# Copying v on VectorE and GpSimd, and reordering the opening of a windowed-attention and gated-MLP kernel

## The chip, the cores and the metric

The kernel runs on one core of a Trainium2 chip. The metric is the device time of one execution in microseconds (us): the median of the timed runs. A core has five engines that work side by side, each through its own instructions in order: TensorE (PE in the profile; PEld are its weight loads), VectorE (DVE), ScalarE (ACT), GpSimd (POOL) and SyncE (SP), whose queue here only starts DMA transfers. PE reads SBUF and writes PSUM banks. GpSimd starts transfers too: all loads that convert f32 to bf16 stand in its instruction stream, between its arithmetic.

## The reference

Sliding-window causal attention (8 batches, 8 heads, 576 positions, 64 per head, window 64), whose output, as 4608 rows of 512, goes through a gated two-layer product:

```python
    scores = scale * np.matmul(q, k.transpose(0, 1, 3, 2))
    rel = pos[:, None] - pos[None, :]
    mask = (rel >= 0) & (rel < window)
    ...
    attn = np.exp(scores - max)
    attn = attn / (np.sum(attn, axis=-1, keepdims=True) + 1e-09)
    x = np.matmul(attn, v)            # heads side by side: 4608 x 512
    h = x @ w_in                      # 512 x 2048
    g = h * np.cos(h)
    return g @ w_out                  # 2048 x 512
```

## The kernel before, in words

**Tiles.** Attention works on units of 64 queries against 128 keys. A unit is (batch b, pair of heads p, block j of 64 positions, 0 to 8). The two heads of a pair lie in partitions 0 to 63 and 64 to 127. Up to four units form a group: groups 0 to 7 are batch 0's blocks 0 to 7 (two groups for each of four pairs, called p.g), group 8 is batch 0's block 8 of all pairs, groups 9 to 16 are batch 1's blocks 0 to 3 (odd numbers) and 4 to 6 (even), two for each pair; 17 and 18 are batch 1's blocks 7 and 8. The gated product works on row tiles of 512 rows; row tile 0 is batch 0's blocks 0 to 7, row tile 1 is group 8 with groups 9 to 16.

**Steps of a group.** Scores on PE (g_scores; L277 writes the mask for the first eight groups, L287 and L293 the products), maximum on VectorE (g_max, L303 and L307), exponentials with their row sums on ScalarE (g_exp, L318), reciprocal on VectorE (g_inv, L325), normalisation on GpSimd or VectorE (g_norm, L332, which writes w), then the transpose of w: by PE and a copy (L341, g_put) for the groups in `direct` (0 to 7, 8, 15, 16), by a DMA transpose that SP issues for the others (L344). `values` (L359) and `values_half` (L378) multiply with v, put_x copies the result to xT.

**v.** load_v (L183) puts 128 positions of v into every second slot of vtiles. A block whose 128 keys straddle two loads needs the odd slots, whose halves are copies from the neighbours. spread_v makes them: for each half of the partitions one strided copy, by an SP DMA (engine "s", L194) or by an engine's copy ("d" VectorE, "p" GpSimd, through `copy`, L132). For batch 0, zA copies slot 1, zB slots 3 and 5, zC slot 7 (each for one or both halves); for batch 1, step y does all at once, y.0 the lower half of the partitions (3 slots) and y.1 the upper (4 slots).

**Order.** Nothing is scheduled by the compiler: the order of the program text is the order on each engine. The string FIRST (L48) writes out the opening by hand, up to about 63 us, and the loop at L534 runs it. Step names: Lq, Lk, Lv, Lwi, Lwo are loads (batch or quarter of the weights, piece); tq, tk transpose batch 0's q and k of a pair on PE, pq, pk copy them out (last letter: the engine, a for ScalarE, d for VectorE, p for GpSimd); Tq, Tk, Pq, Pk the same for batch 1; ms clears a block tile on VectorE; s, m, e, i, n, w, c are the steps of group p.g; Gs, Gm, Ge, Gi, Gn, Gw/Gc, Gp those of a group by number; v and x are values and put_x for half of row tile 0 (x.1.0 is pairs 2 and 3 of the first half); h, S, g are the first product (L392), the sine (L398) and the gate (L404), 16 of each, five PSUM banks between them in turn (the last number of h is the bank); o and oc are quarters of the second product and its copy out (L411); V and X are values and put_x of row tile 1; tb and tb2 load ScalarE's sine and exp tables. Row tile 1 and all later ones run in the loop at L540, into which a planner (`at`, `pump`) mixes the attention of the batches to come. There the first product is L428, the sine L556, the gate L559 and the second product L570.

**Around the change.** GpSimd's stream in the opening is: loads of q and k, loads of v, three of w_in's four quarters (Lwi.0 to Lwi.2), seven normalisations, Lwi.3, the last normalisation n.3.1, then w_out, the rest of batch 1 and q, k of batch 2, mixed with the normalisations of groups 9 to 14 and 8. A load waits until the load eight places before it has landed. SP's stream is: two loads of q and k, the copies zB.0, zB.1, zC (L194), the transposes of w of groups 10 and 9, the copy y.0, the transposes of groups 12, 11, 14, 13, 17, 18, then transposes of batch 2's k (L247).

The steps that the prediction uses: h.0.4 is the first product's first step on the third quarter of w_in, h.0.6 the first on the fourth; V.2 is the values of pair 2 in row tile 1, which needs groups 13 and 14.

Of the kernel before, what the change touches and what calls it, by code (L numbers as in the profile page):

```python
# [10 lines left out]
def _safe_warn(msg, *a, **kw):  # L11
# [37 lines left out]
    "io ms.0.d Lq0.0 Lk0.0 ms.1.d mk cq.d ms.2.d mc ck.a tq.0 Lq0.1 pq.0.d Lk0.1 tk.0 pk.0.a s.0.0.0 "  # L49
    "Lq0.2 tq.1 tk.1 m.0.0 pq.1.a ms.3.d s.0.1.1 Lk0.2 tq.2 pk.1.d s.1.0.2 Lq0.3 Lk0.3 tk.2 s.1.1.3 "  # L50
    "e.0.0 tq.3 m.0.1 Lq1.0 Lk1.0 Lq1.1 pq.2.d pk.2.d Lk1.1 tk.3 m.1.0 s.2.0.4 Lv0.0 Lv0.1 Tq.0 Lv0.2 "
    "pk.3.d m.2.0 e.0.1 pq.3.a i.0.0 e.1.0 Tk.0 s.3.0.0 Tq.1 e.2.0 Lv0.3 Lwi.0 Pq.0.d i.1.0 Lwi.1 m.3.0 "
    "m.1.1 i.2.0 Pk.0.a e.3.0 Lwi.2 Tk.1 n.1.0.p s.2.1.1 Pq.1.d Gs.10.2 m.2.1 Gs.9.4 n.0.0.p Pk.1.a "
    "n.2.0.p i.3.0 e.1.1 w.0.0 zA.0.d w.1.0 c.0.0.d Gs.12.0 w.2.0 n.3.0.p i.0.1 c.1.0.d zA.1.d c.2.0.d "
    "e.2.1 zB.0.s zB.1.s n.0.1.p i.1.1 w.3.0 v.0.0 c.3.0.d x.0.0.a s.3.1.3 Gm.10 v.1.0 m.3.1 i.2.1 "
    "Gs.11.2 Gm.9 Gm.12 n.1.1.p x.1.0.a e.3.1 ms.4.d w.0.1 w.1.1 c.1.1.a i.3.1 h.0.0.1 h.0.1.4 tb "
    "n.2.1.p c.0.1.d Lwi.3 w.2.1 h.0.2.0 n.3.1.p v.0.1 S.0.0 Gm.11 w.3.1 S.0.1 h.0.3.3 Lwo.0 S.0.2 "
    "c.2.1.d c.3.1.d v.1.1 zC.s g.0.0 S.0.3 h.0.4.2 ms.5.d x.0.1.a x.1.1.d h.0.5.1 g.0.1 h.1.0.4 g.0.2 "
    "g.0.3 S.0.4 ms.6.d h.0.6.0 h.1.1.3 S.0.5 S.1.0 Lq1.2 S.0.6 g.0.4 S.1.1 g.1.0 h.1.2.2 Lk1.2 ms.7.d "
    "Lq1.3 h.0.7.4 g.0.5 h.1.3.1 Lv1.0 Lwo.1 g.1.1 S.1.2 h.1.4.3 g.0.6 Lk1.3 S.0.7 h.1.5.0 g.1.2 h.1.6.2 "  # L60
# [13 lines left out]
def kernel(  # L74
# [10 lines left out]
    B, H, S, D = q.shape  # L85
# [45 lines left out]
    def copy(engine, out, in_):  # L131
        {"a": nc.scalar.copy, "p": nc.gpsimd.tensor_copy}.get(engine, nc.vector.tensor_copy)(out, in_)  # L132
# [54 lines left out]
    def spread_v(b, half, engine="p", lo=0, hi=4):  # L187
        vt = vtiles[b % 2]
        hi = min(hi, 4 - (half == 0))
        d = slice(64 * half, 64 * half + 64)  # L190
        of = 2 * lo + 2 * (half == 0)
        to, of = vt[d, 2 * lo + 1:2 * hi:2], vt[d, of:of + 2 * (hi - lo) - 1:2]
        if engine == "s":
            nc.sync.dma_start(out=to, in_=of)  # L194
        else:
            copy(engine, to, of)
# [102 lines left out]
    def g_max(n):  # L299
        s_ps, units = st["s", n], groups[n]  # L300
        negm = att.tile([128, GF], F32, tag="negm", name="negm", bufs=8)
        if n < n_first:
            nc.vector.tensor_reduce(out=negm[:, 0:len(units)], in_=s_ps, op=ALU.max, axis=AX.X, negate=True)  # L303
        else:
            s = att.tile([128, GF, 128], F32, tag="s", name="s", bufs=4)
            for u, (b, p, j) in enumerate(units):
                nc.vector.tensor_tensor_reduce(out=s[:, u], in0=s_ps[:, u], in1=mask[:, 2 - j % 2 if j else 0],  # L307
                                               scale=-scale if b else -1.0, scalar=BIG, op0=ALU.add, op1=ALU.min,
                                               accum_out=negm[:, u:u + 1])
            st["s", n] = s  # L310
        st["m", n] = negm
# [152 lines left out]
    n = n_listed  # L464
# [45 lines left out]
    def spread_first(lo, hi):  # L510
        return lambda i, engine: spread_v(0, i, engine, lo, hi)
# [28 lines left out]
    for mt in range(1, n_mt):  # L540
# [5 lines left out]
        for ff in range(n_ff):  # L546
# [8 lines left out]
            e = ff % 2  # L555
# [54 lines left out]
```

## Time and profile before

| | us |
|---|---|
| median of 3 timed runs (lowest, highest) | 313.28 (312.45, 314.71) |
| the profiled execution | 313.61 |
| its span in the trace | 311.8 |
| PE busy | 296.8 (95%) |
| DVE busy | 230.6 (74%) |
| ACT busy | 236.1 (76%) |
| POOL busy | 191.7 (61%) |

The granted clock of TensorE is full throughout (1.00). In the first 60 us the DMA engines are busy in nearly every slice, and PE's busy share is below 10 in 10 only there: 5.25 of the first 10 us, 7.25 of the next, 9.62, 9.95, 9.54, then 8.24 from 50 to 60. How to read it: a line of the chain gives start, length, engine and line of what the end of the execution waited for at that time; a line of waits gives who waited for whom, the total, how often and the longest; a line of the timeline gives start, length, engine, line, operation and how many were merged. "SPq" rows are the times in which SP issued a transfer, not the transfer.

### The profile page before, as it was taken

The page shows a single profiled execution, that of the slowest core. Times are in us where ns is not written, and L with a number is a line of the kernel's source. Part 1 is how long each engine was busy: PE and PEld are TensorE (multiplying, and loading weights), DVE is VectorE, ACT ScalarE, POOL GpSimd, SP SyncE. Part 2 cuts the span into 40 slices and gives each one's busy share as a digit, 9 for nine tenths or more (in the row PEclk, how much of TensorE's full clock was granted, in tenths as well). Part 3 has the DMA queues.
Part 4 walks back from the last instruction along what each step waited for, and adds up shares of the span by engine and source line. Part 5 has one row for each costly group of instructions (what it writes and reads, how often), then busy time and mean ns, then how long its engine had stood idle before and what let it go on. Part 6 is the DMA issues. An engine that isn't in the chain of part 4 may idle for free.

```text
span 311.8 us, 7954 instructions
## 1 busy us (share of the span) xinstructions
PE 296.8 (95%) x2627; PEld 161.6 (52%) x2659; DVE 230.6 (74%) x877; ACT 236.1 (76%) x785; POOL 191.7 (61%) x227
## 2 busy tenths in 40 slices
PE   3789999799999999999999999999999999999996
PEld 3667844445555455445545545455545554454443
DVE  5898978489777976798579867987698758335801
ACT  5998799486997799769976997699869986116600
POOL 8988576993569678966997699769902850000000
PEclk9999999999999999999999999999999999999999
DMA  7999999999959996999999998999794333011011
GB/s 150 175 212 187 200 178 132 132 162 167 241 82 113 138 235 84 117 116 230 120 105 129 216 138 94 139 230 120 91 135 155 65 80 141 0 69 68 0 67 70
DMA packets 155162, 41.17 MB, mean 132 GB/s; under 512 B 143280, under 2 KB 150384, under 8 KB 155120
## 3 DMA queue, kind: packets, MB, share of 16 engines
q0 software_dynamic: 100192, 18.06, 80.8%
q1 hardware_dynamic: 54784, 22.40, 38.1%
q8 instruction: 21, 0.34, 0.5%
q14 instruction: 21, 0.17, 0.2%
q10 hardware_dynamic: 144, 0.20, 0.2%
HBM read 36.70 MB, written 9.44 MB: 148 GB/s over the span
## 4 chain that ended last, share of the span: by engine, by line
PE 83%; DMA 8%; ACT 3%; POOL 3%; DVE 1%; issue 1%; SPq 1%; POOLq 0%; DVEq 0%; ACTq 0%
PE h_ps L428 34%; PE out_ps L570 34%; DMA w_in<-in_moe_w_in_dram 4%; PE s_ps L287 4%; PE h_ps L392 3%; PE o_ps L359 3%; ACT e L318 2%; PE tq_ps L214 2%; DMA wT<-w 2%; DMA k<-in_k_dram 2%; POOL v L183 1%; PE out_ps L440 1%; PE out_ps L411 1%; DVE s L307 1%; SPq L344 1%
## 5 line engine op out<-in xcount | busy, mean ns | idle before, releaser
L570 PE MATMUL out_ps<-w_out,gT 128*128 128x512 bf16 x482 | 116.1, 379 | 0.8 <-issue 0.2
L428 PE MATMUL h_ps<-xT,w_in 128*128 128x512 bf16 x498 | 115.2, 379 | 1.0
L556 ACT ACTIVATE sin<-h_ps 128x512 f32<-128x512 f32 x128 | 74.0, 598 | 34.0 <-PE h_ps L428 30.8
L318 ACT ACTIVATE e<-s,negm 128x128 f32<-128x128 f32 x256 | 98.7, 388 | 0.7 <-DVE negm L307 0.6
L559 DVE TENSOR_TENSOR gT<-h_ps,sin 128x512 bf16<-128x512 f32 x128 | 81.6, 685 | 21.4 <-ACT sin L556 20.6
L332 POOL TENSOR_TENSOR w<-e,rden 128x512 bf16<-128x512 f32 (+1 forms) x75 | 71.2, 965 | 38.7 <-DVE rden L325 36.9
L428 PEld LDWEIGHTS <-w_in 128*128 128x128 bf16 x512 | 48.6, 98 | 53.9 <-issue 0.4
L570 PEld LDWEIGHTS <-gT 128*128 128x128 bf16 x496 | 45.9, 98 | 44.2
L307 DVE CUSTOM_DVE_ANT_0 s<-s_ps,mask 128x128 f32<-128x128 f32 x256 | 58.5, 286 | 1.2 <-PE s_ps L293 1.0
L318 ACT ACTIVATION_READ_ACCUMULATOR e<-s,negm 128x1 f32 x256 | 48.1, 188 | 0.0
L177 POOL DMA_DIRECT2D q<-in_q_dram x36 | 29.0, 805 | 11.1 <-DMA v<-in_v_dram 4.3
L183 POOL DMA_DIRECT2D v<-in_v_dram x40 | 34.1, 873 | 0.4 <-DMA q<-in_q_dram 0.3
L177 POOL DMA_DIRECT2D k<-in_k_dram x36 | 28.8, 802 | 6.9 <-DMA k<-in_k_dram 5.6
L325 DVE RECIPROCAL rden<-den 128x4 f32<-128x4 f32 (+1 forms) x79 | 13.7, 173 | 21.0 <-ACT e L318 17.2
L132 ACT COPY out_sb<-out_ps 128x512 f32<-128x512 f32 (+1 forms) x18 | 10.2, 565 | 24.5 <-PE out_ps L570 18.4
L287 PEld LDWEIGHTS <-qB 128*128 128x128 bf16 x216 | 17.1, 98 | 14.2
L132 DVE CAST xT<-o_ps 128x512 bf16<-128x512 f32 x24 | 15.6, 677 | 10.8 <-PE o_ps L359 10.8
L132 DVE COPY out_sb<-out_ps 128x512 f32<-128x512 f32 x18 | 12.4, 689 | 13.5 <-PE out_ps L570 12.4
L132 DVE COPY qB<-tq_ps 64x576 bf16<-64x576 bf16 x48 | 21.6, 450 | 0.3
L287 PE MATMUL s_ps<-kT,qB 128*128 128x128 bf16 x216 | 21.9, 219 | 0.0
L307 DVE DVE_READ_ACCUMULATOR2_ANT negm<- 128x1 f32 x256 | 21.3, 83 | 0.0
L132 POOL COPY v<-v 64x1536 bf16<-64x1536 bf16 (+1 forms) x10 | 16.8, 1676 | 0.3
(64 smaller groups left out, 253.2 us busy)
## 6 DMA issues: line engine op xcount, KB each, us to landing
out_dram<-out_sb SPq DMA_DIRECT2D x16, 512.0 KB, 7.8
v<-in_v_dram POOLq DMA_DIRECT2D x32, 128.0 KB, 6.1
q<-in_q_dram POOLq DMA_DIRECT2D x36, 96.0 KB, 8.9
k<-in_k_dram POOLq DMA_DIRECT2D x36, 96.0 KB, 9.0
w_in<-in_moe_w_in_dram POOLq DMA_DIRECT2D x4, 512.0 KB, 9.2
w_out<-in_moe_w_out_dram POOLq DMA_DIRECT2D x4, 512.0 KB, 11.3
wT<-w SPq DMA_TRANSPOSE x68, 4.1
q<-in_q_dram POOLq DMA_DIRECT2D x7, 144.0 KB, 6.2
```

The lines of the kernel that those rows point to most:

```text
L132: {"a": nc.scalar.copy, "p": nc.gpsimd.tensor_copy}.get(engine, nc.vector.tensor_copy)(out, in_)
L177: nc.gpsimd.dma_start(out=st[name, b][:, c].rearrange("p (h d) -> p h d", h=H), in_=src.rearrange("h p d -> p h d"))
L183: nc.gpsimd.dma_start(out=vt.rearrange("p (h d) -> p h d", h=H), in_=v[b, :, c * 128:c * 128 + n, :].rearrange("h p d -> p h d"))
L287: nc.tensor.matmul(out=s_ps[:, u].rearrange("p (a t) -> p a t", a=2), lhsT=qblocks[(b % 2) * PAIRS + p][:, j].rearrange("d h t -> d (h t)" ...
L307: nc.vector.tensor_tensor_reduce(out=s[:, u], in0=s_ps[:, u], in1=mask[:, 2 - j % 2 if j else 0], scale=-scale if b else -1.0, scalar=BIG, ...
L318: nc.scalar.activation(e[:, u], s[:, u], AF.Exp, bias=negm[:, u:u + 1], scale=1.0 if n < n_first else -1.0, accum_out=den[:, u:u + 1])
L325: nc.vector.reciprocal(out=rden[:, 0:len(groups[n])], in_=den[:, 0:len(groups[n])])
L332: (nc.gpsimd if engine == "p" else nc.vector).tensor_tensor(out=w[:, 0:u], in0=e[:, 0:u], op=ALU.mult, in1=rden[:, 0:u].unsqueeze(2).to_br ...
L428: nc.tensor.matmul(out=st["h", ff], lhsT=w_in_sb[:, ks, ff * 128:ff * 128 + 128], rhs=st["xT", mt][:, ks], start=start, stop=stop)
L556: nc.scalar.activation(sin, h_ps, AF.Sin, bias=math.pi / 2.0)
L559: nc.vector.tensor_tensor(out=gt[:, e], in0=h_ps, in1=sin, op=ALU.mult)
L570: nc.tensor.matmul(out=o_ps[e], lhsT=gT[ff // 2][:, ff % 2, ms * 128:ms * 128 + 128], rhs=w_out_sb[:, ff], start=ff == 0, stop=ff == n_ff - 1)
```

## The change

The v copies that SP issued as DMA in the opening become copies on engines: zB.0, zB.1 and zC on VectorE (they stand elsewhere in the string, zB one behind the other's work), y.0 on GpSimd in two pieces, yA (two slots) and yB (one slot), with a normalisation between them. The scores and exponentials of the fourth pair's first group (s.3.0, m.3.0, e.3.0) come before batch 1's first k transposes (Tk.0) and copy; that copy, Pk.0, moves from ScalarE to VectorE. Normalisation n.0.0 stands before Lwi.1; n.1.0, n.2.0 and n.3.0 before Lwi.2. v.0.0 stands before w.3.0, and clearing ms.4 later, among the gates. The instructions after the opening are the same in the same order.

```diff
@@ -49,24 +49,24 @@
     "io ms.0.d Lq0.0 Lk0.0 ms.1.d mk cq.d ms.2.d mc ck.a tq.0 Lq0.1 pq.0.d Lk0.1 tk.0 pk.0.a s.0.0.0 "
     "Lq0.2 tq.1 tk.1 m.0.0 pq.1.a ms.3.d s.0.1.1 Lk0.2 tq.2 pk.1.d s.1.0.2 Lq0.3 Lk0.3 tk.2 s.1.1.3 "
     "e.0.0 tq.3 m.0.1 Lq1.0 Lk1.0 Lq1.1 pq.2.d pk.2.d Lk1.1 tk.3 m.1.0 s.2.0.4 Lv0.0 Lv0.1 Tq.0 Lv0.2 "
-    "pk.3.d m.2.0 e.0.1 pq.3.a i.0.0 e.1.0 Tk.0 s.3.0.0 Tq.1 e.2.0 Lv0.3 Lwi.0 Pq.0.d i.1.0 Lwi.1 m.3.0 "
-    "m.1.1 i.2.0 Pk.0.a e.3.0 Lwi.2 Tk.1 n.1.0.p s.2.1.1 Pq.1.d Gs.10.2 m.2.1 Gs.9.4 n.0.0.p Pk.1.a "
-    "n.2.0.p i.3.0 e.1.1 w.0.0 zA.0.d w.1.0 c.0.0.d Gs.12.0 w.2.0 n.3.0.p i.0.1 c.1.0.d zA.1.d c.2.0.d "
-    "e.2.1 zB.0.s zB.1.s n.0.1.p i.1.1 w.3.0 v.0.0 c.3.0.d x.0.0.a s.3.1.3 Gm.10 v.1.0 m.3.1 i.2.1 "
-    "Gs.11.2 Gm.9 Gm.12 n.1.1.p x.1.0.a e.3.1 ms.4.d w.0.1 w.1.1 c.1.1.a i.3.1 h.0.0.1 h.0.1.4 tb "
-    "n.2.1.p c.0.1.d Lwi.3 w.2.1 h.0.2.0 n.3.1.p v.0.1 S.0.0 Gm.11 w.3.1 S.0.1 h.0.3.3 Lwo.0 S.0.2 "
-    "c.2.1.d c.3.1.d v.1.1 zC.s g.0.0 S.0.3 h.0.4.2 ms.5.d x.0.1.a x.1.1.d h.0.5.1 g.0.1 h.1.0.4 g.0.2 "
-    "g.0.3 S.0.4 ms.6.d h.0.6.0 h.1.1.3 S.0.5 S.1.0 Lq1.2 S.0.6 g.0.4 S.1.1 g.1.0 h.1.2.2 Lk1.2 ms.7.d "
-    "Lq1.3 h.0.7.4 g.0.5 h.1.3.1 Lv1.0 Lwo.1 g.1.1 S.1.2 h.1.4.3 g.0.6 Lk1.3 S.0.7 h.1.5.0 g.1.2 h.1.6.2 "
-    "Lwo.2 g.0.7 S.1.3 S.1.4 S.1.5 Lwo.3 h.1.7.4 Lv1.1 S.1.6 g.1.3 g.1.4 S.1.7 g.1.5 Lv1.2 g.1.6 tb2 "
-    "Tk.2 Lv1.3 Pk.2.d Ge.10 Tq.2 Pq.2.d Tq.3 Ge.9 Ge.12 o.0.0.1 Pq.3.d Tk.3 o.1.0 Pk.3.d Lv0.4 Lq2.0 "
-    "Ge.11 Gs.14.3 Gi.10 Gm.14 g.1.7 Lq2.1 Gs.13.0 Lq2.2 o.0.1.2 Gi.9 o.2.0 Ge.14 Gn.10.p Gm.13 Gc.10 "
-    "Gi.12 Gs.8.3 o.1.1 Gs.16.4 Gm.8 o.3.0 Ge.13 o.2.1 Gs.15.0 Gi.11 oc.0.d Gn.9.p o.3.1 Gn.12.p o.0.2.3 "
-    "Gi.14 Gm.15 Gs.17.1 oc.1.d Gc.9 y.0.s Gn.11.p Gi.13 Gm.16 o.1.2 Ge.8 Ge.16 Ge.15 y.1.d Gn.14.p Gi.8 "
-    "Gc.12 Gm.17 o.0.3.0 Gi.16 Gn.13.p Gc.11 Gn.8.p Lq2.3 Lq2.4 Lq2.5 o.2.2 Gn.16.d Gw.8 Gc.14 Gc.13 "
-    "Lk2.0 Gp.8.d o.3.2 Gi.15 Gw.16 Lk2.1 Ge.17 Lk2.2 o.1.3 Gn.15.d V.0 Gp.16.d oc.2.a Gw.15 Gi.17 Lk2.3 "
-    "o.2.3 V.1 Gp.15.d X.0.a Gn.17.d X.1.d V.2 V.3 X.2.a X.3.d Gc.17 o.3.3 oc.3.a Gs.18.4 Gm.18 Ge.18 "
-    "Lk2.4 Gi.18 Gn.18.d Gc.18 Lk2.5 Lv1.4 "
+    "pk.3.d m.2.0 e.0.1 pq.3.a i.0.0 e.1.0 s.3.0.0 Tk.0 Tq.1 e.2.0 Lv0.3 Lwi.0 m.3.0 Pq.0.d i.1.0 "
+    "n.0.0.p Lwi.1 m.1.1 i.2.0 e.3.0 Pk.0.d Tk.1 n.1.0.p s.2.1.1 Pq.1.d Gs.10.2 m.2.1 Gs.9.4 Pk.1.a "
+    "n.2.0.p i.3.0 e.1.1 w.0.0 zA.0.d w.1.0 c.0.0.d Gs.12.0 w.2.0 n.3.0.p Lwi.2 i.0.1 c.1.0.d zA.1.d "
+    "c.2.0.d e.2.1 n.0.1.p i.1.1 v.0.0 w.3.0 c.3.0.d x.0.0.a s.3.1.3 Gm.10 v.1.0 m.3.1 zB.0.d i.2.1 "
+    "Gs.11.2 Gm.9 Gm.12 n.1.1.p x.1.0.a e.3.1 w.0.1 w.1.1 c.1.1.a i.3.1 h.0.0.1 h.0.1.4 tb n.2.1.p "
+    "c.0.1.d zB.1.d Lwi.3 w.2.1 h.0.2.0 n.3.1.p v.0.1 S.0.0 Gm.11 w.3.1 S.0.1 h.0.3.3 Lwo.0 S.0.2 "
+    "c.2.1.d c.3.1.d v.1.1 g.0.0 S.0.3 h.0.4.2 ms.5.d x.0.1.a x.1.1.d h.0.5.1 g.0.1 h.1.0.4 g.0.2 g.0.3 "
+    "ms.4.d S.0.4 ms.6.d h.0.6.0 h.1.1.3 S.0.5 S.1.0 Lq1.2 S.0.6 g.0.4 S.1.1 g.1.0 zC.d h.1.2.2 Lk1.2 "
+    "ms.7.d Lq1.3 h.0.7.4 g.0.5 h.1.3.1 Lv1.0 Lwo.1 g.1.1 S.1.2 h.1.4.3 g.0.6 Lk1.3 S.0.7 h.1.5.0 g.1.2 "
+    "h.1.6.2 Lwo.2 g.0.7 S.1.3 S.1.4 S.1.5 Lwo.3 h.1.7.4 Lv1.1 S.1.6 g.1.3 g.1.4 S.1.7 g.1.5 Lv1.2 g.1.6 "
+    "tb2 Tk.2 Lv1.3 Pk.2.d Ge.10 Tq.2 Pq.2.d Tq.3 Ge.9 Ge.12 o.0.0.1 Pq.3.d Tk.3 o.1.0 Pk.3.d Lv0.4 "
+    "Lq2.0 Ge.11 Gs.14.3 Gi.10 Gm.14 g.1.7 Lq2.1 Gs.13.0 Lq2.2 o.0.1.2 Gi.9 o.2.0 Ge.14 Gn.10.p Gm.13 "
+    "Gc.10 Gi.12 Gs.8.3 o.1.1 Gs.16.4 Gm.8 o.3.0 Ge.13 o.2.1 Gs.15.0 Gi.11 oc.0.d Gn.9.p o.3.1 Gn.12.p "
+    "o.0.2.3 Gi.14 Gm.15 Gs.17.1 oc.1.d Gc.9 Gn.11.p Gi.13 Gm.16 o.1.2 Ge.8 Ge.16 Ge.15 y.1.d Gn.14.p "
+    "yA.p Gi.8 Gc.12 Gm.17 o.0.3.0 Gi.16 Gn.13.p yB.p Gc.11 Gn.8.p Lq2.3 Lq2.4 Lq2.5 o.2.2 Gn.16.d Gw.8 "
+    "Gc.14 Gc.13 Lk2.0 Gp.8.d o.3.2 Gi.15 Gw.16 Lk2.1 Ge.17 Lk2.2 o.1.3 Gn.15.d V.0 Gp.16.d oc.2.a Gw.15 "
+    "Gi.17 Lk2.3 o.2.3 V.1 Gp.15.d X.0.a Gn.17.d X.1.d V.2 V.3 X.2.a X.3.d Gc.17 o.3.3 oc.3.a Gs.18.4 "
+    "Gm.18 Ge.18 Lk2.4 Gi.18 Gn.18.d Gc.18 Lk2.5 Lv1.4 "
 )
 
 
@@ -522,6 +522,7 @@
              "pq": lambda p, engine: put_q(0, p, engine), "pk": lambda p, engine: put_k(0, p, engine),
              "Pq": lambda p, engine: put_q(1, p, engine), "Pk": lambda p, engine: put_k(1, p, engine),
              "zA": spread_first(0, 1), "zB": spread_first(1, 3), "zC": lambda engine: spread_v(0, 1, engine, 3, 4),
+             "yA": lambda engine: spread_v(1, 0, engine, 0, 2), "yB": lambda engine: spread_v(1, 0, engine, 2, 3),
              "y": lambda half_, engine: spread_v(1, half_, engine),
              "s": lambda p, g, which: g_scores(2 * p + g, which), "m": lambda p, g: g_max(2 * p + g),
              "e": lambda p, g: g_exp(2 * p + g), "i": lambda p, g: g_inv(2 * p + g),
```

## The prediction

> **What bounds the kernel now.** I read the page's shares first, then the chain of waits in order of time, then the waits of PE by stretch, then the timeline of the queue that the chain passes through. All times below are microseconds from the span's start in the one profiled execution (313.61 us, span 311.8; the median of the timed runs, 313.28, lies 0.33 below it).
>
> The page's chain gives 83% to PE and 8% to DMA; the last two lines are PE's waits from 64 us on and its DMA and POOL waits before 65:
>
> ```profile
> PE 83%; DMA 8%; ACT 3%; POOL 3%; DVE 1%; issue 1%; SPq 1%; POOLq 0%; DVEq 0%; ACTq 0%
> ...
> PE out_ps L570 <- issue: 0.2, 1, 0.2
> ...
> PE o_ps L359 <- DMA wT<-w: 1.5, 1, 1.5
> PE out_ps L411 <- DMA w_out<-in_moe_w_out_dram: 0.3, 1, 0.3
> PE h_ps L392 <- DMA w_in<-in_moe_w_in_dram: 0.2, 1, 0.2
> ```
>
> After 64 us PE waits 0.2 us in all, so nothing there can be gained; what the change moves lies before it, and a shift of the point where the second row tile's loop begins (59.9) passes whole to the end. The chain up to there, in order of time (start, length, what):
>
> ```profile
> 13.48 13.31 DMA w_in<-in_moe_w_in_dram
> 26.84 10.65 PE h_ps L392 x96
> ...
> 49.20 1.05 POOL w L332
> 50.25 0.59 SPq L344
> 50.93 1.21 SPq L344
> 52.22 5.68 DMA wT<-w
> 57.95 0.66 PE o_ps L359 x30
> ```
>
> The reader sees two places where PE is released from outside: 26.84, the third part of w_in (waited for 0.2 us), and 57.95, the transposed weights of group 13 (1.5 us). The second is a queue: the normalised tile was done at 50.25, its transpose was issued only at 52.22, because the transposes of groups 12, 11, 14 and 13 go out one behind another at about 1.3 us each from 48.30. Why they begin so late stands in SP's timeline and SP's waits:
>
> ```profile
> 43.78 2.58 SPq L344 DMA_TRANSPOSE wT<-w  x2
> 47.60 0.60 SPq L194 DMA_DIRECT2D v<-v  x1
> 48.30 15.94 SPq L344 DMA_TRANSPOSE wT<-w  x6
> ...
> SPq L194 <- DMA v<-in_v_dram: 16.8, 2, 15.7
> ```
>
> Step y.0.s (batch 1's v, moved by DMA) stands on SP between the second and third transpose and waits for loads of v that land at 47.6. POOL had group 12 ready at 45.5 (four normalisations from 42.91 to 46.52). So SP idles from 46.36 to 47.60 with work behind the wait.
>
> **The change part by part.**
>
> 1. y.0.s leaves SP (one issue, 0.6 us, and its wait for v). Groups 12, 11, 14 go out at 46.4, 47.7, 49.0, group 13 when n.13 is done. Instead POOL runs yA (64x1024) between n.14 and n.13 and yB (64x512) between n.13 and n.8. POOL's rows 64x1536 at 1.458 and 64x2048 at 1.894 give 0.436 per 512 and 0.15 fixed: 1.02 and 0.59. n.14 ends 48.21, yA 49.25 (its v landed by about 46.7), n.13 49.25 to 50.30 against 49.20 to 50.25; yB to 50.9, before n.8's reciprocal is there (n.8 began 51.14). Queued behind yA and yB are n.13, n.8 and the q and k loads of batch 2; they have 0.05 and 0.2 of cover. Group 13's transpose is then issued at 50.3, 1.9 earlier. Its landing took 5.7, its two predecessors' 3.8, the first ones' 6.7: 54.1 to 57.0, and I take 56. PE finishes V.1 at 56.45. So V.2 starts at 56.45 to 57.05 instead of 57.95: 1.46 gained, 0.9 at the worst end. Behind it X.2, X.3, o.3.3, the last scores and exps, the sine table and the loop follow one another on the chain and shift with it; the q and k of batch 2 that the loop needs land by 59 and 64, and the first scores on the transposed k come at 75.0, about 1 us after its third chunk (issued 66.9, 7.2 to land). If that cover fails the cost is tenths.
>
> 2. zB.0, zB.1 and zC leave SP and DMA (320 KB, issues 17.35 to 20.09). SP gains nothing there: its next work waits until 43.78. The DMA engines are saturated: w_in's first three parts land at 20.2, 22.9 and 26.8 and the fourth at 29.4, some 2.6 apiece, and 3.9 where these copies lie between. So the loads behind them land about 1.1 earlier. That removes PE's wait for w_out (0.3 at 45.04, ahead of oc.0, i.14, i.13, i.8); k of batch 1 (0.42 at 39.36) is worth nothing, since the k copy behind it is held by VectorE. Gain 0.3, bounds 0 to 0.7.
>
> 3. VectorE takes zB.0, zB.1 (64x1024 each), zC (64x512) and Pk.0 (row 0.74). Rows 64x512 at 0.25 and 0.34 and 64x2048 at 1.09 give about 0.56 for 64x1024. ms.4 (0.54) moves from before i.3.1 to between the gates. ScalarE loses Pk.0 (0.68) and its 0.44 wait for m.3.0, since s.3.0 (10 matmuls) now runs at 12.5 on PE, ahead of Tk.0's 18 transposes and of the 1.58 in which PE waited at 12.6. So ScalarE is 1.1 ahead at e.1.1. That lead does not reach PE: VectorE's own row, placed end to end (m.3.0 at 13.15, then 0.60, Pq.0 0.65, 0.08, m.1.1 0.60, 0.08, Pk.0 0.65, Pq.1 0.65, m.2.1 0.60), brings i.3.0 to 17.06 against 17.48, 0.4 earlier only.
>
> 4. POOL: n.0.0 goes ahead of w_in's second part, n.1.0 to n.3.0 ahead of the third. Parts are issued at 14.2 and 18.4 instead of 12.75 and 13.5; the fourth, behind zB.0's 0.56 through i.2.1 and n.2.1, at 22.9 instead of 22.26. n.3.0 ends 18.37 (before 18.75), but the part's issue (0.78) then stands ahead of n.0.1 and n.1.1, which ends 21.25 against 20.81; w.1.1 waits for it and the first h matmuls start at 21.6 against 21.49. The interruptions behind are shorter (v.0.1 no longer waits for a DMA copy), so PE comes to h.0.4 at about 26.45, if the third part has landed. Parts took 7.1 to 13.3 from issue, the longer the more lay ahead in the queue. At 18.4 the second still has 4 us to go, so I take 7.1 to 8.2: 25.5 to 26.6. Fourth: by the queue 28.4, by 7.1 us 30.0, needed at 29.1: 0 to 0.85, and I take 0.
>
> 5. Then PE runs the h matmuls at 0.87 each, with VectorE's gates behind. VectorE idles 0.5 there (its waits for the sines) and gets ms.4 and zC, 0.84. Walked through, g.0.5 frees bank X0 at 33.0 where h.1.3 wants it at 32.7: 0.3 lost, which eats the 0.3 to 0.4 of item 4. Items 3 to 5 together 0, bounds -0.4 to +0.9. v.0.0 ahead of w.3.0 costs w.3.0 0.3 and is in the walk.
>
> 6. The copies on VectorE beside GpSimd. Two equal copies took 0.25 and 0.34: the first with POOL between instructions, the second with a normalisation starting beside it; and y.1 (64x2048, 49.69 to 50.78) ended 0.53 after n.13 did. A reading of these rows is that such a copy waits until GpSimd's instruction ends and then runs fast. In that case y.1 and yB meet at 50.3: y.1 first costs n.8 0.3, yB first 0.6. Without it 0. I take 0.3, as the row of y.1 is nearest, ends 0 and 0.6. The Trainium skill, "SBUF — State Buffer", section "Who interferes with whom", says this outright: a VectorE copy in a two-port mode and a GpSimd instruction take one port pair in turn, each for its whole length. By that rule every new copy waits for a normalisation; without it the three small rows are only their sizes. The trace's two equal copies and y.1 agree with it, but also fit a plain per-element price.
>
> Sum: -1.46 (1) -0.3 (2) +0 (3 to 5) +0.3 (6) = -1.46, so 312.15 for the profiled execution and 311.8 against the median.
>
> **The rivals.**
>
> *Eaten.* Each new VectorE copy waits out a normalisation of 1.04 (item 6 in full): zB.0 at 21.0 holds i.2.1 and with it n.2.1, w.2.1 and the fourth part of w_in by another 0.5, the gates 0.3, n.8 0.6. For it: POOL is busy without a gap from 17.7 to 22.3, where zB lands. Against: POOL's normalisations have one length (1.042) whatever runs beside. Sum: -1.46 - 0.3 + 0.5 + 0.3 + 0.6 = -0.4, 312.9.
>
> *Late weights, slower than before.* The third part of w_in keeps its 13.3 from issue to landing: 18.4 + 13.3 = 31.7, PE stands at h.0.4 for 4.9 longer than before, items 1 and 2 give 1.5 back: +3.4, 316.7. It decides for slower from a landing at 28.3 (26.84 + 1.46), 9.9 after issue. For it: issue is 4.9 later and three of w_out's four parts took 10.8 to 12.2. Against: part four took 7.1, with the queue as full.
>
> *More.* ScalarE's lead and the lighter DMA bring x.1.0 and the h stage 0.5 forward, with no bank stall, both 0.3 and 0.42 waits of item 2 go, and n.8 is not late: -1.46 - 0.7 - 0.6 = -2.8, 310.5. Against: VectorE is already 9.1 of 10 us busy from 20 to 30.
>
> *Not what it says:* if n.13 or PE's own order, not SP, held V.2, the time would stay; speaking against it is n.13's end 1.97 before its transpose was issued. It is in the first rival's share.
>
> **How the numbers follow.** Forecast (311.2 to 312.6) 0.52; eaten or no effect (312.6 to 314.0) 0.22; more (below 311.2) 0.13; late weights 0.13. The predicted time is the first's, 311.8. The range 310.4 to 314.0 takes in the bounds of items 1 to 6 and leaves out the late weights and a sliver of "more". A measurement tells about 1% (3.1 us) from no change: below 310.15 only the end of "more", 0.04; above 316.4 most of "late weights", 0.10; the rest, 0.86, within.
>
> **What would show it.** Right: in SP's timeline no v copy at 47, third transpose at 46.4, the last of the four at 50.3; PE's wait for wT gone or below 0.5; h matmuls running through from about 26.5. Wrong: PE waiting for w_in at h.0.4 or at 29 (item 4); VectorE copies of v of 0.8 or more beside normalisations, n.8 ending after 52.5 (item 6); PE waiting for gT in the h stage by more than 0.3 (item 5); a wait for the transposed k near 75 (item 1).

## The result, and the profile after

The changed kernel is slower by a little: 314.06 us median of 22 runs (313.29 to 317.07) against 313.01 of the kernel before (22 runs, 311.44 to 315.28), ratio 1.0049 [1.0034, 1.0065]. That is within the 1% that was called no change, but on the other side of it: +1.1 where -1.46 was forecast, and 0.06 above the range.

The profiled execution of after took 313.53 (span 311.8). That is 0.1 less than the profiled execution of before (313.61), so the two profiles do not show the difference that the medians show. A second profile of the kernel before (run before_b: 312.34, span 310.6) lies nearer to what before usually does, and it is used beside the first one below. Timed runs also differ in the clock that TensorE was granted (an average of 0.995 or less in 14 of before's 35 runs on the chip of after_same, which is the changed kernel timed again below, and in none of after_same's 12); among the others the medians are 312.25 and 314.14, so the clock is not what made the change slower.

The page of after gives VectorE a place on the chain that it did not have (1% before); the other lines are PE's waits from 59 us on, all of them, and two of those ahead of it:

```profile
PE 82%; DVE 9%; POOL 2%; ACT 2%; DMA 2%; issue 2%; SPq 0%; DVEq 0%; POOLq 0%; ACTq 0%
```

```profile
PE o_ps L359 <- DMA wT<-w: 0.3, 1, 0.3
PE h_ps L428 <- DVE xT L132: 0.2, 1, 0.2
PE out_ps L571 <- issue: 0.2, 1, 0.2
```

```profile
PE h_ps L392 <- DVE gT L404: 0.4, 1, 0.4
...
PE h_ps L392 <- DMA w_in<-in_moe_w_in_dram: 0.2, 1, 0.2
```

V.2's wait of 1.5 for wT is gone. In its place PE waits for gT in the gates' stretch, and there is a wait for wT and one for xT after 59, where before had only 0.2 of issue. Before's chain from 13 to 37 was one DMA piece and one run of PE. In after the same stretch of the chain (start, length, what) is VectorE, link by link:

```profile
23.52 1.14 DVE v L132
...
25.61 0.67 DVE wT L132 x2
26.28 0.60 DVE gT L404
...
28.02 1.79 DVE gT L404 x3
...
29.88 0.54 DVE qB L508
...
30.49 0.54 DVE qB L508
31.03 1.14 DVE gT L404 x2
...
32.20 0.29 DVE v L132
...
32.66 0.54 DVE qB L508
...
33.95 4.53 PE h_ps L392 x40
```

The reader sees the second half of zB at 23.52 (1.14 long), two clears one behind the other at 29.88 (ms.4 has come to stand beside another), zC at 32.20, and then PE released by the gate g.0.5 at 33.95. PE's own rows show the two stops, 0.18 for the fourth part of w_in and 0.38 for the gate; the third part, feared late, held nothing:

```profile
26.65 3.07 PE L392 MATMUL h_ps<-xT,w_in 128*128 128x256 bf16 x24
29.90 3.67 PE L392 MATMUL h_ps<-xT,w_in 128*128 128x256 bf16 x32 [0.18 <-DMA w_in<-in_moe_w_in_dram]
33.95 4.53 PE L392 MATMUL h_ps<-xT,w_in 128*128 128x256 bf16 x40 [0.38 <-DVE gT L404]
```

What the first step promised did happen. SP's timeline has no v copy any more, GpSimd does the two pieces, and PE runs V.1 to V.3 through:

```profile
43.66 14.54 SPq L344 DMA_TRANSPOSE wT<-w  x7
```

```profile
48.78 1.03 POOL L132 COPY v<-v 64x1024 bf16<-64x1024 bf16 x1
49.83 1.04 POOL L332 TENSOR_TENSOR w<-e,rden 128x512 bf16<-128x512 f32 x1
50.81 1.07 POOL L132 COPY v<-v 64x512 bf16<-64x512 bf16 x1
51.85 1.03 POOL L332 TENSOR_TENSOR w<-e,rden 128x512 bf16<-128x512 f32 x1
```

```profile
56.72 0.95 PE L359 MATMUL o_ps<-wT,v 128*64 128x64 bf16 x48
```

**Where the time went.** This table cuts each profiled execution at four starts on PE: the first product with w_in (L392), the first transpose of k behind the gates (L211), the loop (L428) and the last rows (L440); the four columns behind the first are lengths of stretches (differences of starts, worked out from the traces).

| kernel | first product at | gates' stretch | to the loop | loop to last rows | rest | span |
|---|---|---|---|---|---|---|
| before | 21.49 | 15.93 | 22.43 | 245.26 | 6.73 | 311.8 |
| before_b | 21.66 | 15.85 | 21.05 | 245.26 | 6.74 | 310.6 |
| after | 21.68 | 16.73 | 20.50 | 245.89 | 6.95 | 311.8 |
| after_same | 21.55 | 16.73 | 20.51 | 245.88 | 6.93 | 311.6 |
| y_only | 23.03 | 15.64 | 20.51 | 245.26 | 6.76 | 311.2 |
| y_order | 21.93 | 15.70 | 20.51 | 245.26 | 6.77 | 310.2 |
| order_only | 21.74 | 16.74 | 20.43 | 245.26 | 6.73 | 310.9 |
| zB_only | 20.92 | 16.53 | 20.44 | 245.85 | 6.83 | 310.6 |
| z_only | 22.84 | 16.51 | 20.43 | 245.87 | 6.88 | 312.5 |
| before_dve | 23.34 | 15.47 | 20.43 | 246.01 | 6.73 | 312.0 |
| late_clears | 22.43 | 15.91 | 20.58 | 246.01 | 6.94 | 311.9 |
| clears_pool | 21.94 | 15.82 | 21.58 | 245.26 | 6.94 | 311.5 |
| loads_later | 21.44 | 15.86 | 20.43 | 245.26 | 6.74 | 309.7 |

The first column varies by over 2 us. Part of that is TensorE's clock: from 20 to 25 us the granted clock was 0.68, 0.75 and 0.69 in y_only, z_only and before_dve, the three latest of the table, and 1.00 in the other ten; the same eight score products (L293) took 0.63 in z_only (at 20.58) and 0.39 in after (at 19.30). The other ten still lie between 20.92 and 22.43, so a single profile says little about a median. The stretches behind it repeat better, the loop's to hundredths. After against before_b: gates +0.88, to the loop -0.55, loop +0.63, rest +0.21, first product 0: +1.2, which is the medians' +1.05 within 0.2. Against the first profile of before the second term is -1.93, and that is why the two profiles agree. So there are three things to explain: why the gates' stretch grew, why the gain ahead of the loop is 0.55 and not 1.46, and why the loop, in which not one instruction was moved, grew by 0.6.

### The profile page after: what moved, and what is told of

Read it like the earlier page. It is cut to its first block, busy times and chain, and to the rows that moved or that the text cites. A ratio compares the mean times of both kernels' runs of the same rounds, so it can differ in the third digit from the quotient of the medians.

```text
span 311.8 us, 7949 instructions
## 1 busy us (share of the span) xinstructions
PE 297.3 (95%) x2627; PEld 161.6 (52%) x2659; DVE 233.4 (75%) x881; ACT 235.4 (76%) x784; POOL 193.5 (62%) x229
## 4 chain that ended last, share of the span: by engine, by line
PE 82%; DVE 9%; POOL 2%; ACT 2%; DMA 2%; issue 2%; SPq 0%; DVEq 0%; POOLq 0%; ACTq 0%
PE h_ps L428 34%; PE out_ps L571 31%; PE s_ps L287 4%; PE out_ps L411 3%; PE o_ps L359 3%; PE tq_ps L214 2%; DVE negm L303 2%; PE h_ps L392 1%; DVE gT L404 1%; DVE v L132 1%; PE out_ps L440 1%; DVE s L307 1%; POOL w L332 1%; POOL v L132 1%; DMA rows<-in_k_dram 1%
## 5 line engine op out<-in xcount | busy, mean ns | idle before, releaser
L428 PE MATMUL h_ps<-xT,w_in 128*128 128x512 bf16 x498 | 115.2, 379 | 1.1 <-DVE xT L132 0.2
L428 PEld LDWEIGHTS <-w_in 128*128 128x128 bf16 x512 | 48.6, 98 | 54.0 <-issue 0.6
L132 DVE COPY qB<-tq_ps 64x576 bf16<-64x576 bf16 x48 | 21.6, 450 | 0.3
L132 POOL COPY v<-v 64x1536 bf16<-64x1536 bf16 (+3 forms) x12 | 18.8, 1570 | 0.3
```

The source lines that it names most:

```text
L428: nc.tensor.matmul(out=st["h", ff], lhsT=w_in_sb[:, ks, ff * 128:ff * 128 + 128], rhs=st["xT", mt][:, ks], start=start, stop=stop)
```

## The experiments

All kernels are timed against the kernel before on the same chip, in five rounds where nothing else is said. The diffs are of the hand-written order of steps.

**The change in its three parts.** after_same is the changed kernel as it is. y_only, z_only and order_only are the kernel before with one part each:

```diff
 y_only      -y.0.s   +yA.p behind Gn.14.p   +yB.p behind Gn.13.p
 z_only      -zB.0.s -zB.1.s -zC.s   +zB.0.d behind m.3.1   +zB.1.d behind c.0.1.d
             +zC.d behind g.1.0   ms.4.d moved behind g.0.3
 order_only  the rest: s.3.0 ahead of Tk.0, Pk.0.d, n.0.0 to n.3.0 among Lwi, v.0.0 ahead of w.3.0
```

> The changed kernel once more, for a second profile beside its parts. Both theories: 0.5 to 1.5 us slower than the kernel before. In the trace: first product's stage ends near 38.4 (before 37.5), PE's wait for the transposed weights ahead of V.2 gone; if the start of the loop at 59 differs from the first profile by more than 0.3, one profile is not enough to read a part from.

> Only batch 1's y.0 goes from SP's DMA to GpSimd (yA, yB); all else as before. Theory A (the gain of freeing SP is real, the VectorE copies and the late quarters of w_in lose more than that in the first product's stage): 0.5 to 1.5 us faster, V.2 without a wait, first product's stage ending at 37.5 as before. Theory B (freeing SP gains nothing that lasts, because GpSimd with yA and yB runs its later work 0.7 late and that is waited for further on): -0.2 to +0.8 us, and waits of PE after 64 us that the kernel before has not.

> Only batch 0's copies zB and zC go from SP's DMA to VectorE, and the clearing ms.4 moves among the gates; all else as before. Theory A: 0.5 to 1.2 us slower: VectorE is behind with the gates, PE waits for a bank near h.1.3, the first product's stage ends at 38.0 to 38.6. Theory B: within 0.3 us of the kernel before, stage end 37.3 to 37.7.

> Only the order: fourth pair's scores and exps ahead of batch 1's k, Pk.0 on VectorE, normalisations among w_in's loads, v.0.0 ahead of w.3.0; all v copies as before. Theory A: 0 to 0.6 us slower, by PE's wait for the third or fourth quarter of w_in (landing 25.5 to 26.6 and 28.4 to 30). Theory B: within 0.3 us either way.

Measured: after_same 314.14, ratio 1.0043 [1.0013, 1.0072]; y_only 312.59, 0.9997 [0.9979, 1.0014]; z_only 314.24, 1.0049 [1.0023, 1.0076]; order_only 312.43, 0.9986 [0.9955, 1.0018]; before 312.65. The whole loss comes with z_only's part, batch 0's copies on VectorE and the clear that moved with them. Batch 1's copy on GpSimd and the new order are each no change that can be measured. For y_only neither theory came true: it is not 0.5 faster or more, and after 64 us PE waits no more than in before (0.2).

**Which of VectorE's new items, and before a second time.**

```diff
 zB_only   -zB.0.s -zB.1.s   +zB.0.d behind m.3.1   +zB.1.d behind c.0.1.d     (from before)
 zB_early  zB.1.d moved up, directly behind zB.0.d                              (from after)
 y_order   zB.0, zB.1, zC and ms.4 as in before                                 (from after)
```

> The kernel before once more, for a second profile. Theory C (the wait of 1.5 us ahead of V.2 in the first profile is slack made by an early opening: the transposes are tied to when v lands, the opening varies by over a microsecond from execution to execution, so on most executions PE comes to V.2 when the weights are there and y has nothing to gain): first product starts later than 21.49, at 22.5 to 23.1, and the wait ahead of V.2 is below 0.5. Rival D (the wait is there every time, and y's gain is paid back elsewhere): the wait is 1.2 to 1.7 again, wherever the first product starts.

> The kernel before with zB.0 and zB.1 alone on VectorE; zC stays a DMA and ms.4 stays ahead of i.3.1. Theory A1 (a VectorE copy of v waits for the GpSimd normalisation beside it: 64x1024 takes 0.4 alone and 1.1 to 1.25 beside one, and this late row holds the gates): 0.8 to 1.5 us slower, zB.1 at 1.1 or more. Theory A2 (the load is ms.4 and zC among the gates): within 0.4 us of the kernel before.

> The changed kernel with zB.1 moved directly behind zB.0, where GpSimd waits for the reciprocal of n.2.1 and normalises nothing. Theory A1: zB.1 takes 0.3 to 0.5 instead of 1.13, VectorE comes to the gates 0.5 to 0.8 earlier, and the kernel is 0.4 to 0.9 us faster than the changed one (so 0.6 to 1.1 slower than before). Theory A2: no different from the changed kernel, 1.2 to 1.6 slower than before.

> The change without its VectorE copies: y on GpSimd and the new order, zB and zC as DMA, ms.4 in its old place. Theory C: like y alone and the order alone, 0 to 0.5 us faster than before. Rival D: 1.0 to 1.5 faster, if y and the order repair different waits. First product starts at 21.6, PE waits about 1.2 for zB.1's DMA ahead of v.0.1.

Measured: before_b, one run, 312.34; zB_only 314.07, 1.0044 [1.0024, 1.0063]; zB_early 314.12, 1.0027 [1.0006, 1.0049]; y_order 312.45, 0.9984 [0.9961, 1.0007]; before 312.71. The two copies zB alone carry the loss; zC and ms.4 add nothing to it that the medians show. How long the copies take is in VectorE's rows, of zB_only, of z_only and of zB_early:

```profile
20.59 0.41 DVE L132 COPY v<-v 64x1024 bf16<-64x1024 bf16 x1
23.50 1.09 DVE L132 COPY v<-v 64x1024 bf16<-64x1024 bf16 x1
```

```profile
21.86 0.41 DVE L132 COPY v<-v 64x1024 bf16<-64x1024 bf16 x1
24.35 1.25 DVE L132 COPY v<-v 64x1024 bf16<-64x1024 bf16 x1
```

```profile
21.52 1.02 DVE L132 COPY v<-v 64x1024 bf16<-64x1024 bf16 x2
```

The same copy costs 0.41 or 1.09 to 1.25; the last row is both copies together, 0.58 and 0.42. In after they are 0.58 (from 20.74) and 1.13 (from 23.52), and GpSimd's rows there tell why:

```profile
18.99 2.04 POOL L332 TENSOR_TENSOR w<-e,rden 128x512 bf16<-128x512 f32 x2
21.49 1.04 POOL L332 TENSOR_TENSOR w<-e,rden 128x512 bf16<-128x512 f32 x1 [0.46 <-DVE rden L325]
...
23.30 1.05 POOL L332 TENSOR_TENSOR w<-e,rden 128x512 bf16<-128x512 f32 x1
```

The first copy ends at 21.32, 0.3 after the normalisation that ends at 21.03; the second at 24.65, 0.3 after the one that ends at 24.35. Each stands still until GpSimd is done and then takes its own 0.3 to 0.4: the price is what is left of the normalisation when the copy comes. In zB_only the product that needs it waits for it directly:

```profile
24.64 0.44 PE L378 MATMUL o_ps<-wT,v 128*64 128x64 bf16 x16 [0.56 <-DVE v L132]
```

In after the copy's 0.6 too much shifts the gates instead, and ms.4 and zC come on top: the same length of stretch (16.5 to 16.7) by two ways. zB_early saves 0.7 of the copies' time, yet its median is that of after within the intervals, and not the 0.4 to 0.9 less that theory A1 expected. Its profile is of an execution of 317.02, whose loop alone lost 3 us, mostly to waits for wT, but its opening shows where the saving goes:

```profile
23.61 1.03 PE L392 MATMUL h_ps<-xT,w_in 128*128 128x256 bf16 x8 [0.48 <-DVE negm L307]
...
34.58 4.53 PE L392 MATMUL h_ps<-xT,w_in 128*128 128x256 bf16 x40 [0.42 <-DVE gT L404]
```

PE now waits for maxima that stand behind both copies on VectorE. It waits at g.0.5 as well, although VectorE stood idle for 0.71 (until PE's next transpose of w) just ahead of the gates: so the clear ms.4 and zC among the gates hold PE there without any lateness from the copies.

**A wait in the loop that nothing was moved for.** In the traces of all five kernels with zB on VectorE, and in none of the others so far, PE waited for wT at 122 us, as here in zB_only:

```profile
120.91 0.89 PE L359 MATMUL o_ps<-wT,v 128*64 128x64 bf16 x44
122.23 0.55 PE L359 MATMUL o_ps<-wT,v 128*64 128x64 bf16 x20 [0.43 <-DMA wT<-w]
```

SyncE issues seven transposes of w from about 110 to 123 us. The last three take 2.3, 2.4 to 2.5 and 2.9 to 3.2 us from issue to landing in the kernels without the wait, 2.3 to 2.4, 3.0 to 3.2 and 2.5 in those with it. The late one has a packet of the DMA queue that the profile calls instruction in its flight. Two kernels ask whose packet that is, and two more take the clears out of the gates:

```diff
 before_dve   before, with three one-element VectorE clears ahead of Gi.18 (60 us)
 zB_again     zB_only, with zB.0.s zB.1.s once more behind v.1.1
 late_clears  after, ms.4.d ms.5.d ahead of Gi.18, ms.6.d ms.7.d behind Gn.18.d, zC.d ahead of oc.0.d
 clears_pool  after, ms.4.p to ms.7.p behind Lv0.4, zC.d ahead of oc.0.d
```

> The kernel before with three one-element VectorE clears of a tile that nothing reads, put where VectorE idles (at some 60 us); nothing else is changed. In all traces so far one of the seven transposes of w that SyncE issues at 110 to 123 us lands 0.7 us later than its like (3.1 instead of 2.4), and a packet of 8,192 bytes of the DMA queue called instruction falls into its flight; in the kernels without a v copy on VectorE in the opening it is the seventh, in those with one the sixth, and PE then waits 0.4 there. Theory A, the packet is VectorE's, and its place goes by how many instructions VectorE has had: with three more it falls on the sixth here too, PE waits 0.4 at 122, and the time is 0.3 to 0.6 above before (ratio 1.001 to 1.002). Theory B, its place goes by what SyncE has issued: no wait at 122, ratio 1.000.

> zB_only (the two halves of batch 0's blocks 1 and 2 copied by VectorE), and SyncE copies the same rows to the same place once more, behind the opening's last product with v: SyncE issues what it issues in the kernel before, VectorE what it issues in zB_only. Theory A (place by VectorE's count): the sixth transpose still lands late, PE waits 0.4 at 122, ratio as zB_only's, 1.0035 to 1.0050. Theory B (place by SyncE's issues): the seventh lands late again, no wait, and 0.4 to 0.5 us less than zB_only, ratio 1.0020 to 1.0030. In both, PE's wait of some 0.5 for VectorE's second copy at 24.6 stays.

> The kernel after, with VectorE's four clears ms.4 to ms.7 (0.54 each) and its copy zC moved out of the gates' stretch, to idle moments at 45 and 60 us. Theory 1, what the change loses in the opening is VectorE's work among the gates: the waits of PE for gT (0.4 to 0.6) and the ends that follow are gone, the stretch from the first product with w_in to the first transposes of batch 1's k falls from 16.7 to 15.8 to 16.2, and the time by 0.5 to 0.9 (ratio to before 1.002 to 1.003; the wait at 122 stays). Theory 2, the loss there lies in the two copies zB themselves (each beside or behind a normalisation): nothing changes by over 0.2, ratio 1.004 to 1.005.

> As late_clears, but ms.4 to ms.7 are GpSimd's, behind its last load of batch 0's v, where it idles (37 to 42 us): VectorE has four instructions fewer than in the kernel after, about as many as in the kernel before. Theory 1 with A: the gates' stretch as in late_clears, and no wait at 122 either: 0.4 to 0.5 less than late_clears, ratio to before 0.9995 to 1.0015. Theory 1 with B: as late_clears, 1.002 to 1.003. Theory 2 with A: 1.003; with B: 1.0045. Against all of them: GpSimd's clears delay batch 2's loads or its first normalisation at 42.8, and the time goes up by what PE then waits at 53 to 58.

Measured: before_dve 313.27, 1.0017 [0.9992, 1.0041]; zB_again 314.51, 1.0080 [1.0051, 1.0108]; late_clears 313.49, 1.0036 [1.0009, 1.0062]; clears_pool 313.01, 1.0019 [0.9990, 1.0048]; before 312.45.

Theory A holds in every trace. Three clears of one element each, 0.33 us of VectorE's idle time in all, bring the wait at 122 into the kernel before, and the packet is there (the first fence is PE's rows in before_dve, the second its DMA queues between 121.5 and 122.5; columns packets, MB, share):

```profile
122.26 0.89 PE L360 MATMUL o_ps<-wT,v 128*64 128x64 bf16 x44
123.77 0.55 PE L360 MATMUL o_ps<-wT,v 128*64 128x64 bf16 x20 [0.62 <-DMA wT<-w]
```

```profile
q1 hardware_dynamic: 514, 0.13, 129.1%
q14 instruction: 1, 0.01, 2.1%
```

zB_again, whose SyncE issues what it issues in before, keeps the wait (0.59); clears_pool, whose VectorE has four instructions fewer than after, loses it, and all 64 products run through:

```profile
122.36 1.21 PE L359 MATMUL o_ps<-wT,v 128*64 128x64 bf16 x64
```

Over all sixteen profiles the rule has no exception. The count is VectorE's on the page of each profile; the landings are of the sixth and seventh transpose:

| VectorE instructions | kernels | sixth | seventh | wait at 122 | loop to last rows |
|---|---|---|---|---|---|
| 876 to 878 | before, before_b, y_only, order_only, y_order, loads_later, y_order_late, clears_pool | 2.42 to 2.46 | 2.73 to 3.16 | none | 245.26 (y_order_late 245.88: a wait of 0.6 for gT) |
| 879 to 881 | before_dve, zB_only, zB_again, z_only, after, after_same, late_clears, zB_early | 2.96 to 3.34 | 2.46 to 2.57 | 0.28 to 0.62 | 245.85 to 246.01 (zB_early 248.24) |

PE needs the sixth at once and the seventh later, so the loop is 0.6 to 0.75 longer with the lateness in one place and as long as ever with it in the other (in after and late_clears about 0.2 of it are waits for xT and gT elsewhere). In the medians this term alone is not resolved (before_dve's interval holds 1); the traces resolve it. The Trainium skill, "Runtime: NRT & Kernel Launch", section "Instruction fetch mechanics", says that each engine's instructions come in blocks over a DMA queue of its own, and that crossing a block boundary is "mostly hidden". The traces agree as far as they go (21 packets in queue q14 on the page of after, 0.17 MB together, one of them seen to cost); the case shows what the word mostly leaves open. Why a single packet of 0.3 to 0.9 us delays a transpose by 0.5 to 0.9 no run here shows.

late_clears answers the other question: with the clears and zC out of the gates the stretch is 15.91 again, as before's, though the second copy still takes 1.37 there. So the gates' stretch grew because VectorE had the copies on top of the clears, and without the clears it has room for them. (PE also comes 1.1 later to w_in's fourth part in that execution than in after, and does not wait for it, so not all of the 0.82 is the clears'.) The moved clears cost something where they went: PE's wait of 0.2 for gT in the loop's first gates. clears_pool has 15.82 and no wait at 122, but its four clears hold GpSimd for 4.09 us, and PE then waits 1.2 for a normalisation at 53: the case that the expectation named against all theories. zB_again is dearer than either theory said; its stretch to the loop is 21.80, with V.2 waiting 0.96 for wT.

**The first step's 1.46.** That wait at V.2 is a race. SyncE's last transpose of that set and GpSimd's first load of batch 2's q are issued at about the same time. In the profiles in which batch 1's copy is SyncE's:

| kernel | transpose ahead of the load by | lands after | V.2 waits |
|---|---|---|---|
| before | -0.10 | 5.68 | 1.46 |
| zB_again | 0.11 | 5.40 | 0.96 |
| before_b | 0.47 | 5.24 | 0.43 |
| before_dve | 0.92 | 3.36 | - |
| zB_only | 1.12 | 3.10 | - |
| order_only | 1.60 | 3.16 | - |
| z_only | 1.62 | 3.20 | - |

With yA and yB on GpSimd the transpose goes out earlier and the loads later, the lead is 1.5 to 1.9, it lands in 2.4 to 3.2, and no profile shows the wait. Four of the kernels in the table have none either, with the copy still on SyncE: it was not SyncE's copy alone that made PE wait. A kernel that moves the loads and leaves SyncE's copy tells the race from the copy; with it went the version that the runs pointed to:

```diff
 loads_later   before, ms.4 as ms.4.p directly ahead of Lq2.3 (GpSimd, 1.06 us)
 y_order_late  y_order, ms.4.d to ms.7.d as in late_clears
```

> The kernel before, with one clear (ms.4, VectorE's at 23 us) done by GpSimd right ahead of its loads of batch 2's last three q chunks (1.0 us in clears_pool's trace): the loads come 1 us later, SyncE's work is untouched. Theory R, the wait of V.2 is a race between the last transpose of that set and those loads: the transpose is 0.9 to 1.5 ahead of the loads, lands 2.5 to 3.4 after its issue instead of 5.2 to 5.7, PE doesn't wait at V.2, and the time is 0.3 to 0.9 below before (ratio 0.997 to 0.999), or the same if before mostly wins the race. Theory S, SyncE is late by the v copy that it issues ahead of those transposes: the wait stays at 0.4 to 1.5, ratio 1.000.

> The kernel after with batch 0's copies back on SyncE's DMA queue (as y_order), and VectorE's four clears moved behind the gates as in late_clears. If VectorE's clears among the gates cost nothing there, as PE's waits in y_order say (0.2 for w_in, none for gT): as y_order, ratio 0.9970 to 0.9995, no wait at V.2, none at 122 (VectorE's count is y_order's). If they cost 0.3 or more: 0.996 or less.

Measured: loads_later 312.87, 1.0012 [0.9988, 1.0037]; y_order_late 313.25, 1.0030 [0.9998, 1.0063]; before 312.54. In loads_later the lead is 1.37, the transpose lands in 4.5 (less than 5.2, more than the 2.5 to 3.4 expected), and PE's products run through, so in this one execution the wait goes with the loads while SyncE's copy stays, as theory R says. The lead does not settle the landing by itself (1.37 here landed later than 0.92 in before_dve), and PE waited 1.46 and 0.43 in the two profiles of before, so one profile without the wait is weak evidence. The time does not fall: 1.0012, where 0.997 to 0.999 was expected, or no change if before mostly wins the race.

y_order_late is not better than y_order either, and its 1.0030 is above what either case of its expectation allowed. Its profile (315.44) shows the copies' price once more, at the two zA copies that VectorE had all along: 0.25 to 0.34 each in before, 1.56 and 1.07 here (VectorE's rows, then GpSimd's):

```profile
16.92 1.56 DVE L132 COPY v<-v 64x512 bf16<-64x512 bf16 x1
...
19.24 1.07 DVE L132 COPY v<-v 64x512 bf16<-64x512 bf16 x1
```

```profile
15.29 3.04 POOL L332 TENSOR_TENSOR w<-e,rden 128x512 bf16<-128x512 f32 x3
...
19.10 1.05 POOL L332 TENSOR_TENSOR w<-e,rden 128x512 bf16<-128x512 f32 x1
```

The first ends 0.15 after three normalisations in a row, the second 0.16 after a fourth. PE waits 1.1 for what is queued behind the first and 1.2 for the second, and its first product with w_in begins at 24.32, later than in any other profile. The granted clock was 0.50 there from 20 to 25 us as well, so how much of the late start is the copies' and how much the clock's is not separated. Neither copy was touched by the edit: where they fall among GpSimd's work is a matter of the execution (0.25 to 0.97 over the other fifteen profiles), and it is another source of the first column's spread. What the edit did cost stands in the loop: two of the moved clears run on VectorE from 64.62 to 65.76, the loop's first gate begins behind them at 65.68, and PE waits 0.60 for it at 66.36. The DMA copies that the change took away have a spread of their own: in order_only the second zB, issued at 18.29, lands 7.56 later (5.8 to 6.8 in y_order, before_b and y_order_late), and PE waits for it (the row names ScalarE, which had long been done):

```profile
25.94 0.44 PE L378 MATMUL o_ps<-wT,v 128*64 128x64 bf16 x16 [1.20 <-ACT sin L398]
```

No kernel of these is measurably faster than the kernel before; y_order comes nearest, at 0.9984 [0.9961, 1.0007].

## Why the prediction was wrong, point by point

In short: the 1.46 that step 1 was to gain was the length of one execution's wait, worth 0.55 against a second profile of before and nothing in y_only's median; and the gates (step 5, taken as 0) and the loop (in no step) lost 0.88 and 0.63. Of the prediction's own signs of being wrong four came: a wait for w_in at 29.9 (0.18), a copy of 1.13 beside a normalisation, n.8 ending at 52.88, and a wait of 0.38 for gT; only the wait near 75 did not.

1. *y.0.s leaves SP, -1.46.* Each of its marks came: transposes issued without the gap, the last of the four at 50.9 (forecast 50.3), the wait gone, yA 1.03 (1.02). The size was wrong, and with it the reason: the prediction put V.2's wait down to SP's late issue, but order_only, zB_only, z_only and before_dve have y.0.s on SP and no wait; how long the last transpose takes to land, beside GpSimd's loads, decides too. The 1.46 was the wait of one execution of a race; the second profile of before had 0.43 of it, and y_only, with the wait gone, is 312.59 against 312.65, its interval allowing 0.65 of gain at most. In the stretch to the loop the step is worth 2.0, 0.55 or nothing, by how the race went in the execution that one compares with. How often before loses it is not settled by these runs. This is the step that failed first.
2. *SP and DMA relief, -0.3.* The wait for w_out is not in after, but not in before_b either. It was no property of the kernel: 0.
3. *ScalarE's lead does not reach PE.* Right: the first product begins at 21.68 (forecast 21.6), and order_only is 0.9986.
4. *w_in's parts.* Right: the products run from 26.65 (forecast 26.5) with no wait for the third part, and the fourth costs 0.18 to 0.39 (taken 0, bounds 0 to 0.85). The rival *late weights* is ruled out by that row.
5. *Gates, net 0 with bounds -0.4 to +0.9.* The value taken was wrong, the upper bound right: +0.88 against before_b. The stall at g.0.5 was foreseen at 33.0 with 0.3 and came at 33.95 with 0.38; what was missed is that VectorE came to the gates late already, by the copy of 1.13. That is not the whole of it: zB_early, where it did not, has a stop of 0.42 at the same gate, from the clear and zC alone.
6. *The copies beside GpSimd, 0.3.* By the row it is 0.41 alone, 0.58 where it touches a normalisation, 1.09 to 1.37 beside one, not 0.56 each. GpSimd pays the same: yB took 1.07 beside y.1 (forecast 0.59), and n.8 began at 51.85 instead of 51.14, for which PE waited 0.17. The Trainium skill's rule ("SBUF — State Buffer", section "Who interferes with whom") agrees with all of these rows, and the price per element that the prediction weighed against it does not. With step 5 this makes the part of the loss that lies in the opening.
7. *"A shift of the point where the second row tile's loop begins passes whole to the end."* It does in every kernel with 878 VectorE instructions or fewer whose loop has no other wait (245.26 to the hundredth), and not in after: 0.63 is lost; the views show 0.29 of it as PE's wait at 122 and 0.2 as a wait for xT whose cause no run isolates. The term was not in the sum at all.

The sum by what was measured against before_b: -0.55 (1) +0 (2 to 4) +0.88 (5 and 6) +0.63 (7) +0.21 (the rest behind the last rows, where no run isolates a cause) = +1.2. Against the kernels that keep y.0.s on SP and have no wait (20.43 to the loop) step 1 is +0.07 and the same sum +1.8; the medians of the runs at full clock, given with the result, differ by 1.9. That, and y_only and loads_later being no faster than before, speaks for before mostly having no wait; it is an estimate. Of the rivals, *eaten* had the right mechanism and the nearest time, but put the price mainly on w_in and n.8 (0.5 and 0.6, where PE waited 0.18 and 0.17), kept the whole 1.46 as a gain and knew nothing of the loop.

## What to carry to other kernels

A wait that stands in one profile is worth what it is on the average of executions: take a second profile of the kernel before, compare the granted clock of the stretch, and look whether the wait is a race of two queues, before its length goes into a sum. A copy that leaves a DMA queue for VectorE is priced at its row beside a GpSimd instruction, not at its size, and it comes on top of whatever VectorE does for PE there. When instructions are added to one engine, stretches far behind can change without any edit; compare their lengths between traces, and where they differ, look for the instruction packets among the transfers that PE waits for.

## What the runs showed of the hardware that was not expected

- Three one-element clears on VectorE at 60 us made a DMA transpose at 120 us land 0.9 later (3.34 against 2.42 to 2.46), by moving a packet of the instruction queue; PE lost 0.62 to it.
- A transpose issued on SyncE less than 0.5 ahead of a GpSimd load landed in 5.2 to 5.7 us, one issued 0.9 to 1.6 ahead in 3.1 to 4.5, one issued 1.5 to 1.9 ahead, in the kernels with yA and yB, in 2.4 to 3.2.
- A VectorE copy of 64x512 took between 0.25 and 1.74, by how much of GpSimd's normalisations was ahead of it; not one alone, but all that followed without a gap (1.74 in clears_pool: zC, begun at 45.67, ended at 47.41, 0.16 after the last of four normalisations in a row).
- The clear of a 128x576 tile that takes VectorE 0.54 takes GpSimd 1.02 to 1.06.
- Lengths between fixed points of PE repeat to 0.01 us over kernels and executions in the loop (245.26, in seven profiles of six kernels), while the start of the first product varies from 20.9 to 24.3.
- Four profiles have a granted TensorE clock of 0.50 to 0.75 between 20 and 25 us and 1.00 from 40 us on; their first product begins at 22.8 to 24.3, in the other twelve at 20.9 to 22.4.
